# Routing logits taken out of the output product: VectorE sums of finished rows, TensorE for the last four tiles

## The chip, the cores and the metric

The kernel runs on one core of a Trainium2 chip, as one program. The metric is the device time of one execution in microseconds (us), lower is better; the figure for a kernel is the median of its runs.

## The reference, cut to what matters

Three stages follow each other over 3072 tokens of width 384. An attention recurrence (4 batches, 8 heads of 48, 768 steps) gives `x`; a gated layer of inner width 1536 follows; then a top-1 mixture of 8 experts of inner width 1024.

```
x = (sigmoid(x @ w_gate) * (x @ w_val)) @ w_out                  # 384 -> 1536 -> 384
xn = x / (norm(x) + 1e-6);  en = expert_emb / (norm(expert_emb) + 1e-6)
logits = xn @ en.T / tau                                          # 8 logits for each token
expert_idx = argmax(logits);  gate_w = softmax(logits)[expert_idx]
out = gate_w * (relu(x @ w1[expert_idx]) @ w2[expert_idx])
```

What matters here are the 8 logits of each token: they are inner products of the finished row `x` with the 8 normalised embeddings.

## The kernel before, in words

**Tokens and groups.** The 3072 tokens are 24 chunks of 128. Two chunks make a group of 256 tokens; there are 12 groups, 0 to 11. Attention is done chunk by chunk. Groups 0 and 1 are done one at a time (`emit_gv`, tiles `pgv`), groups 2 to 11 in five pairs of 512 tokens (`emit_wide`, tiles `pgate`, `pval`, 512 columns a product).

**The gated layer.** The inner width is cut into 12 blocks f. For each block of a pair TensorE makes the gate (9 matmuls, L730) and the value (9 matmuls, L730); VectorE multiplies with the sigmoid (`sgw`, L743), ScalarE rounds the product to a high part (`gth`, L745), VectorE subtracts for the low part (`gtl`, L747). One block later `emit_out` (L767 to L777) multiplies with the output weights `wo` and adds into the PSUM tiles `o`, 6 matmuls for a group, 12 for a pair, over all 12 blocks. Here "step" means one block of a pair: gate, value, and the output product of the block before. A step has two ticks; the stages of attention for the chunks ahead are hung on ticks by the table `stages` (6 ticks a chunk).

**Where the logits come from.** `wo` holds for each block 384 output columns and 8 more: w_out times the normalised embeddings. So the 392-column output product gives the row and its 8 logits together. To make the 8 columns, `conv` transposes each unit of output weights on TensorE (`ptw`, L446; ScalarE copies them, L447) and multiplies the transposes with the embeddings (`pg`, L457; copied at L461, L462). That happens six times, in the first 126 us.

**The early stage.** Up to 163 us the chunks 0 to 8, groups 0 and 1, and the conversion of 18 units of 64-bit weights (`conv`: two ScalarE passes, two VectorE passes, a rounding and a subtraction) are emitted by a planner: each is a generator that says when it wants to be emitted (`CHUNK_AT`, `CONV_AT`, `GV_AT`, ...), and whether it needs a temporary tile (`avail["x"]`). The tables do not depend on how long anything takes.

**Routing.** When a group's 12 blocks are summed, `route_pick` (L779) copies the 8 logits and the row from PSUM (tile `xr`), sums the squares on ScalarE (L799), and finds the expert on VectorE. `route_rank` (L803) counts, with three small matmuls `pr`, how many tokens went to each expert before, and scatters the rows (`xs`, L818, by GpSimd's indirect DMA) to the experts' regions in DRAM. `first_rows` (L882) counts what each expert has up to the last pair, sorts the experts, and loads the first 336 rows of one expert, which `first_xT` (L899) transposes and `first_h` (L911) uses right after the last pair: eight hidden blocks of 9 matmuls of 336 columns that cover the last rows' way through DRAM. Then 112 more rows (`x`, L1356) come back from DRAM, are transposed (L1363) and used (L1368), and the experts' products `y` (L1286) follow.

**Queues.** SP issues the loads in program order: `ld` and `ldr` are the attention chunks (three buffers: two of `ldp`, one of `r2p`; chunk c + 3 is loaded when chunk c is done with, L360), `raw` the 64-bit weights, `wraw` the experts' weights.

Of the kernel before, what the change touches and what calls it, by code (L numbers as in the profile page):

```python
# [8 lines left out]
F32 = mybir.dt.float32  # L9
# [13 lines left out]
RW = 400  # L23
# [18 lines left out]
AT_ROWS = 5  # L42
# [5 lines left out]
IN_ORDER = 16.12  # L48
EMB_AT = 20.18
WARM = 12  # L50
WARM_WIDE = 6
# [8 lines left out]
def kernel(  # L60
# [33 lines left out]
    xs = dram.tile([E * REGION, RW], F32, name="xs")  # L94

# [31 lines left out]
    def wtile(nm):  # L127
        return wp.tile([P, 1568], F32R, tag="w", name=nm)
# [170 lines left out]
    if True:  # L299
# [54 lines left out]
        def load_chunk(c):  # L354
            if c % 3 == 2:
# [42 lines left out]
        def load_unit(n):  # L398
            kind, i = units[n]
            w = wp.tile([P, 768], I64, tag="w", name="raw", padded_shape=[P, 784])  # L400
# [13 lines left out]
        def conv(n):  # L414
# [23 lines left out]
            wv = w.rearrange("p (f l c) -> p f l c", f=2, l=2)  # L438
            xv = x.rearrange("p (f c) -> p f c", f=2)
            nc.scalar.activation(wv[:, :, 0, 0:384], xv, AF.Copy)  # L440
            yield CONV_T[2], ("x", 1)
# [7 lines left out]
            lo.tensor_tensor(wv[:, :, 1, 0:384], xv, wv[:, :, 0, 0:384], op=ALU.subtract)  # L449
            avail["x"] += 1  # L450
            yield CONV_T[4], "en"

            pgs = ps_gv.tile([P, 2, P // E, E], F32, tag="gv", name="pg")
            pg = pgs[:, :, 0]
            for f in range(2):
                for k in range(3):
                    nc.tensor.matmul(  # L457
                        pgs[:, f], xT[:, f, k, :], enT[:, k, :].unsqueeze(1).to_broadcast([P, P // E, E]),
                        start=(k == 0), stop=(k == 2),
                    )  # L460
            nc.scalar.activation(wv[:, :, 0, 384:392], pg, AF.Copy)  # L461
            nc.vector.tensor_tensor(wv[:, :, 1, 384:392], pg, wv[:, :, 0, 384:392], op=ALU.subtract)  # L462
# [4 lines left out]
        embt = tmpp.tile([E, DM], F32, tag="x", name="embt")  # L467
        nc.sync.dma_start(out=embt, in_=emb)
        taut = c1.tile([E, 1], F32, name="taut")
        nc.sync.dma_start(out=taut, in_=tau.broadcast_to([E, 1]))  # L470
# [25 lines left out]

        def embeddings():
            esq = tmpp.tile([E, DM], F32, tag="x", name="esq")
# [9 lines left out]
            nc.vector.tensor_scalar(embt, embt, es[:, 5:6], None, op0=ALU.mult)  # L508
            pe = ps_gv.tile([P, 3, E], F32, tag="gv", name="pe")
# [211 lines left out]
        scores = {}  # L721

# [56 lines left out]
        def route_pick(g):  # L779
            xr = rtp.tile([P, 2 * RW], F32, tag="xr", name="xr").rearrange("p (t c) -> p t c", t=2)  # L780
            sq = tmpp.tile([P, DM], F32, tag="x", name="sq")
            lg = xr[:, :, 384:392]
            for t in range(2):
                nc.scalar.activation(lg[:, t], po[g][t][:, 384:392], AF.Copy)
# [10 lines left out]
            nc.gpsimd.memset(xr[:, :, 394:RW], 0.0)  # L795
            nc.gpsimd.tensor_copy(xr.bitcast(I32)[:, :, 393], tokid[:, 2 * g:2 * g + 2])
            for t in range(2):
# [211 lines left out]
        def rank_due(n):  # L1009
            for r in ranks:  # L1010
                r[0] -= 1
# [496 lines left out]
```

## Time and profile before

| | |
|---|---|
| median of 3 runs | 832.94 us (832.31 to 834.7) |
| the profiled execution | 836.85 us, its span 835.1 us, granted TensorE clock 0.982 |
| TensorE busy | 811.8 us, 97% of the span |
| VectorE busy | 414.5 us, 50% |
| ScalarE, GpSimd busy | 323.2 us (39%), 213.2 us (26%) |
| DMA | 99.85 MB, mean 120 GB/s |

Busy time is the union of an engine's instructions. The chain of waits follows the work that ended last back in time; its pieces are listed in order of time. A tile's name stands left of the arrow, what it is made from on the right. Clock figures are shares of 2.4 GHz.

### The profile page before, as it was taken

Reading aid. Unit: us, or ns where it says so; the run is one execution under the profiler, and the core shown is the slowest. Engines: PE = TensorE matmul, PEld = TensorE weight load, DVE = VectorE, ACT = ScalarE, POOL = GpSimd, SP = SyncE. Lnnn points to the kernel's source line nnn. Section 1 sums busy time; section 2 is a strip of 40 time slices with the busy share of each in tenths; the row PEclk is TensorE's granted clock in tenths of the full one; section 3 lists DMA queues with packets and bytes.
Section 4 is the critical chain, followed back from the end, with each engine's and each line's share of the span. In section 5 each row is a group of like instructions: output and inputs, shape, how many; then the busy total and the mean of one; then the engine's idle time right before and its main releaser. Section 6 shows DMA issues by size and latency. Waiting matters only on the chain.

```text
span 835.1 us, 16946 instructions
## 1 busy us (share of the span) xinstructions
PE 811.8 (97%) x6955; PEld 727.0 (87%) x6955; DVE 414.5 (50%) x913; ACT 323.2 (39%) x698; POOL 213.2 (26%) x247
## 2 busy tenths in 40 slices
PE   6899989999999999999999999999999999999997
PEld 5788989878888888888888888888999998899997
DVE  7998764533334333434353324343474554556650
ACT  6586743311223212321231224333364454555541
POOL 5612023653333433335141100100210102102202
PEclk8699999999999999999999999999999999999999
DMA  9568733312121222122211001610366466465401
GB/s 355 196 240 289 236 118 113 137 41 67 58 68 58 86 78 67 58 87 77 68 58 30 21 10 57 195 61 20 105 215 222 131 218 229 128 219 160 143 11 54
DMA packets 35357, 99.85 MB, mean 120 GB/s; under 512 B 4337, under 2 KB 18401, under 8 KB 32329
## 3 DMA queue, kind: packets, MB, share of 16 engines
q1 hardware_dynamic: 31639, 88.77, 31.6%
q0 software_dynamic: 3632, 9.93, 3.3%
q8 instruction: 56, 0.92, 0.4%
q14 instruction: 28, 0.23, 0.1%
q10 hardware_dynamic: 2, 0.00, 0.0%
HBM read 80.94 MB, written 16.27 MB: 116 GB/s over the span
## 4 chain that ended last, share of the span: by engine, by line
PE 76%; issue 12%; DMA 4%; DVE 3%; POOL 2%; ACT 1%; another core or an unknown queue 0%; POOLq 0%; SPq 0%; ACTq 0%
PE o L775 18%; PE pval L730 15%; PE pgate L730 15%; PE y L1286 7%; PE ph L924 7%; PE pgv L730 4%; PE py L647 3%; DMA ldr<-in_att_dram 2%; PE py L627 2%; DMA ld<-in_att_dram 2%; POOL out_dram L1329 1%; PE pg L457 1%; PE py L604 1%; PE pt L1251 1%; PE ph L1368 1%
## 5 line engine op out<-in xcount | busy, mean ns | idle before, releaser
L730 PE MATMUL pval<-xt,gv 128*128 128x512 f32 x540 | 135.8, 395 | 0.0
L730 PE MATMUL pgate<-xt,gv 128*128 128x512 f32 x540 | 134.6, 393 | 0.0
L775 PE MATMUL o<-wo,gth 128*128 128x392 f32 x480 | 128.2, 348 | 0.0
L730 PEld LDWEIGHTS pval<-xt,gv 128*128 128x128 f32 x540 | 100.2, 188 | 22.3 <-issue 0.4
L924 PE MATMUL ph<-xk,we 128*128 128x384 f32 (+6 forms) x576 | 116.9, 350 | 0.0
L730 PEld LDWEIGHTS pgate<-xt,gv 128*128 128x128 f32 x540 | 100.7, 188 | 18.0
L743 DVE TENSOR_TENSOR sgw<-pval,sgw 128x512 f32<-128x512 f32 x60 | 41.5, 691 | 139.3 <-PE pval L730 132.7
L924 PEld LDWEIGHTS ph<-xk,we 128*128 128x128 f32 x576 | 102.8, 188 | 6.0 <-issue 1.2
L1286 PE MATMUL y<-we,ht 128*128 128x384 f32 (+1 forms) x528 | 102.0, 340 | 0.0
L745 ACT ACTIVATE gth<-sgw 128x512 fp32r<-128x512 f32 x60 | 37.9, 632 | 146.8 <-DVE sgw L743 139.5
L739 ACT ACTIVATE sgw<-pgate 128x512 f32<-128x512 f32 x60 | 36.3, 605 | 146.8 <-PE pgate L730 138.1
L1286 PEld LDWEIGHTS y<-we,ht 128*128 128x128 f32 (+1 forms) x528 | 92.1, 187 | 1.0
L775 PEld LDWEIGHTS o<-wo,gth 128*128 128x128 f32 x480 | 87.6, 190 | 4.3
L775 PE MATMUL o<-wo,gtl 128*128 128x392 f32 x240 | 82.3, 343 | 0.0
L1329 POOL DMA_INDIRECT out_dram<-yo,xrow x26 | 26.6, 1022 | 173.6 <-ACT yo L1326 161.5
L747 DVE TENSOR_TENSOR gtl<-sgw,gth 128x512 fp32r<-128x512 f32 x60 | 46.7, 778 | 37.9 <-ACT gth L745 37.2
L844 DVE TENSOR_TENSOR we<-wraw,we 128x768 fp32r<-128x768 f32 x64 | 61.0, 957 | 8.3 <-ACT we L841 6.4
L929 DVE SCALAR_TENSOR_TENSOR ht<-ph,ht 128x384 fp32r<-128x384 f32 (+1 forms) x56 | 31.9, 569 | 64.6 <-ACT ht L928 60.1
L928 ACT ACTIVATE ht<-ph 128x384 fp32r<-128x384 f32 (+1 forms) x56 | 28.2, 503 | 85.6 <-PE ph L924 79.8
L730 PE MATMUL pgv<-xt,gv 128*128 128x256 f32 x432 | 59.0, 289 | 0.0
L730 PEld LDWEIGHTS pgv<-xt,gv 128*128 128x128 f32 x432 | 55.8, 194 | 0.4
L841 ACT ACTIVATE we<-wraw 128x768 fp32r<-128x768 f32 x64 | 53.3, 838 | 5.6 <-PE pval L730 2.9
(251 smaller groups left out, 1073.3 us busy)
## 6 DMA issues: line engine op xcount, KB each, us to landing
wraw<-in_wex_dram SPq DMA_DIRECT2D x64, 384.0 KB
ld<-in_att_dram SPq DMA_DIRECT2D x15, 1152.0 KB
raw<-in_wgv_dram SPq DMA_DIRECT2D x12, 768.0 KB
ldr<-in_att_dram SPq DMA_DIRECT2D x8, 1152.0 KB
w2f<-in_wex_dram SPq DMA_DIRECT2D x8, 768.0 KB
xs<-zt SPq DMA_DIRECT2D x8, 750.0 KB
raw<-in_wout_dram SPq DMA_DIRECT2D x6, 768.0 KB
xrow<-xs SPq DMA_DIRECT2D x6, 600.0 KB
```

The lines of the kernel that those rows point to most:

```text
L730: nc.tensor.matmul(pg, a, x[:, k, b, :], start=(n == 0), stop=(n == 8))
L739: nc.scalar.activation(sg, p0, AF.Sigmoid)
L743: nc.vector.tensor_tensor(sg, p1, sg, op=ALU.mult)
L745: nc.scalar.activation(hi, sg, AF.Copy)
L747: q = nc.vector.tensor_tensor(lo, sg, hi, op=ALU.subtract)
L775: nc.tensor.matmul(po[g][t], gt[a][:, ts_], w[:, f % 2, b, :], start=(f == 0 and n == 0), stop=(f == NF - 1 and n == 2))
L841: q = nc.scalar.activation(w[:, 0:768], r, AF.Copy)
L844: nc.vector.tensor_tensor(w[:, 768:1536], r, w[:, 0:768], op=ALU.subtract)
L924: nc.tensor.matmul(ph, a, x[:, k, b, :], start=(n == 0), stop=(n == 8))
L929: nc.vector.scalar_tensor_tensor(ht[:, 1, :], ph, 0.0, ht[:, 0, :], op0=ALU.max, op1=ALU.subtract)
L1286: nc.tensor.matmul(yo[e, t], ht[:, a, :], b, start=(f == 0 and n == 0), stop=(f == XF - 1 and n == 2))
L1329: q = nc.gpsimd.indirect_dma_start(out=out, out_offset=bass.IndirectOffsetOnAxis(ap=xrow[e][t].bitcast(I32)[:, 393:394], axis=0), in_=o, i ...
```

## The change

- `wo` loses the 8 columns; `emit_out` multiplies with 384 columns, and `conv` of an output unit makes no transposes and no products with the embeddings.
- `embeddings` loads its input itself, later (`EMB_AT` 20.18, then `EMB_T` 6.0), and writes the normalised embeddings to DRAM (`embd`). After the early stage SP loads them back to all 128 partitions (`embb`, 8 x 384 numbers a partition, into the third chunk buffer). From chunk 9 on the chunks have two buffers, and are loaded two chunks ahead.
- For groups 0 to 9, `route_rows` copies the row and sums the squares, and `route_dots` queues 16 VectorE products with a sum (128 x 384, `scalar_tensor_tensor` with `accum_out`: one for each of two tiles and eight experts), then the pick. Each tick takes some from that queue by the table `DOTS`: 10 in 6 ticks, in the last pair 4 in each tick. The first of a tick is held behind all earlier VectorE work.
- For groups 10 and 11 the rows are transposed on TensorE (`pty`, 12 transposes) and multiplied with the embeddings (`pl`, 12 matmuls of 8 columns), between the blocks of `first_h`; their ranks come after block 3.
- `first_rows` stands at block 7 of the last pair in place of 5, when all earlier groups have been ranked.

```diff
-AT_ROWS = 5
+AT_ROWS = 7
+RANK = 1
+DOTS = ((2, 3, 3, 2, 0, 0), (4, 4, 4, 4, 4, 4))
...
-            xT = tmpp.tile([P, 2, 3, P], F32, tag="x", name="xT")
-            for f in range(2):
-                pt = ps_gv.tile([P, 3, P], F32, tag="gv", name="ptw")
-                for k in range(3):
-                    nc.tensor.transpose(pt[:, k, :], xv[:, f, k * P:(k + 1) * P], ident)
-                nc.scalar.activation(xT[:, f], pt, AF.Copy)
...
-            pgs = ps_gv.tile([P, 2, P // E, E], F32, tag="gv", name="pg")
...
+            nc.sync.dma_start(out=embd, in_=embt)
...
-                po[g] = [ps_o.tile([P, 392], F32, tag=f"o{g % 2}{t}", name=f"o{t}") for t in range(2)]
+                po[g] = [ps_o.tile([P, DM], F32, tag=f"o{g % 2}{t}", name=f"o{t}") for t in range(2)]
...
+        def route_dots(g):
+            xr = route_rows(g)
+            for i in range(2 * E):
+                t, e = divmod(i, E)
+                dots.append(lambda t=t, e=e: nc.vector.scalar_tensor_tensor(
+                    prod, xr[:, t, 0:DM], 1.0, embb[0][:, e], op0=ALU.mult, op1=ALU.mult,
+                    accum_out=xr[:, t, 384 + e:385 + e],
+                ))
+            dots.append(lambda: ranks.append([tick + RANK, route_pick(g, xr)]))
...
+        def AFTER(c):
+            return 3 if c < EARLY else 2
...
+        t = r2p.tile([P, 3072], F32, tag="r2", name="embb")
+        nc.sync.dma_start(out=t, in_=embd.rearrange("e c -> (e c)").partition_broadcast(P))
...
+            n = min(DOTS[tick >= 24 * (len(WIDE) - 1)][tick % 6], len(dots))
...
         for f in range(XF):
             first_h(f)
+            if f == 0:
+                turned = [route_turn(xr, t, n) for n, (g, t, xr) in enumerate(tiles)]
+            elif f == 1:
+                for n, (g, t, xr) in enumerate(tiles):
+                    route_logits(xr, t, n, turned[n])
+                picks = [route_pick(g, xr) for g, xr in ends]
+            elif f == 3:
+                for p in picks:
+                    route_rank(*p)
```

Three places of the order show what moves. The first is SP's queue at the end of the early stage, first before, then now (`xt` are small copies of attention results, `ld` and `ldr` chunks):

```order
L360 DMA ld<-in_att_dram 128x2304
L360 DMA ldr<-in_att_dram 128x2304
L710 DMA xt<-xp_204 16x2x256 x3
L360 DMA ld<-in_att_dram 128x2304 x2
L710 DMA xt<-xp_204 16x2x256 x6
```

```order
L364 DMA ld<-in_att_dram 128x2304
L1140 DMA embb<-embd 128x3072
L700 DMA xt<-xp_203 16x2x256 x3
L364 DMA ld<-in_att_dram 128x2304 x2
L700 DMA xt<-xp_203 16x2x256 x6
```

The embeddings' load takes the place of a chunk's, behind the load of another chunk.

The second is VectorE in the third step of the last pair (`sgw` and `gtl` belong to the gated layer, `we` is the split of an expert's weights, `rs` a pick), first before, then now:

```order
L743 TENSOR_TENSOR sgw<-pval,sgw 128x512
L747 TENSOR_TENSOR gtl<-sgw,gth 128x512
L844 TENSOR_TENSOR we<-wraw,we 128x768
```

```order
L734 TENSOR_TENSOR sgw<-pval,sgw 128x512
L786 SCALAR_TENSOR_TENSOR prod,xr<-xr,embb 128x384 x2
L864 TENSOR_TENSOR we<-wraw,we 128x768
L738 TENSOR_TENSOR gtl<-sgw,gth 128x512
L786 SCALAR_TENSOR_TENSOR prod,xr<-xr,embb 128x384 x4
L813 TENSOR_REDUCE rs<-xr 128x2
L786 SCALAR_TENSOR_TENSOR prod,xr<-xr,embb 128x384
L815 TENSOR_TENSOR rs<-xr,rs 128x16
```

Seven sums and two operations of a pick now stand between two products of the gated layer.

The third is TensorE behind the last output product, up to the transposes of the 112 rows (`ph` are blocks of `first_h`, `pr` the ranks), first before, from the first rank, then now, from the first block:

```order
L807 MATMUL pr<-cum_97,ones 128x16
L924 MATMUL ph_6280<-xk,we 128x336 x3
L808 LDWEIGHTS U
L808 MATMUL pr<-oh,U 128x16
L809 LDWEIGHTS ones
L809 MATMUL pr<-oh,ones 128x8
L924 MATMUL ph_6280<-xk,we 128x336 x4
```

```order
L945 MATMUL ph_6252<-xk,we 128x336 x9
L795 MATMUL pty<-ident,xr 128x128 x6
L945 MATMUL ph_6288<-xk,we 128x336 x5
L795 MATMUL pty<-ident,xr 128x128 x6
L945 MATMUL ph_6288<-xk,we 128x336 x4
L806 MATMUL pl<-enT,yT 128x8 x12
L945 MATMUL ph_6335<-xk,we 128x336 x9
L945 MATMUL ph_6347<-xk,we 128x336 x9
L827 LDWEIGHTS ones
L827 MATMUL pr<-cum_98,ones 128x16
```

The ranks stood inside the first two blocks; now transposes, logits and four blocks come ahead of them, and 12 products `y` stand between the last block and the transposes of the 112 rows, where one did.

## Rows read from the trace of the kernel before

**Rows 1.** The page's part 1: busy us, share of the span, instructions.

```profile
PE 811.8 (97%) x6955; PEld 727.0 (87%) x6955; DVE 414.5 (50%) x913; ACT 323.2 (39%) x698; POOL 213.2 (26%) x247
```

**Rows 2.** Busy time by stretch: us, then PE, PEld, DVE, ACT, POOL, clock, DMA.

```profile
40.00:50.00 10.00, 9.59 (x97) 8.84 (x95) 9.55 (x16) 9.33 (x22) 2.58 (x2) 1.00 0.68 264
...
90.00:100.00 10.00, 10.00 (x74) 9.75 (x73) 7.82 (x14) 6.78 (x15) 0.94 (x1) 1.00 0.80 263
...
300.00:400.00 100.00, 100.00 (x910) 85.92 (x908) 38.24 (x87) 23.80 (x56) 39.19 (x38) 1.00 0.19 63
```

**Rows 3.** The chain of waits, early stage: start us, us, what.

```profile
72.78 0.55 PE ptw L446 x3
...
73.85 1.36 PE pg L457 x12
...
88.56 1.34 PE pg L457 x12
...
101.28 0.87 PE pg L457 x6
...
103.13 0.86 PE pg L457 x6
...
121.32 0.55 PE ptw L446 x3
...
123.15 2.66 PE pg L457 x12
```

**Rows 4.** Stretch by instructions of tile pg: PE, PEld, DVE, ACT, clock, DMA.

```profile
121.00:126.00 5.00, 2.73 (x12) 2.54 (x12) 0.00 (x0) 0.15 (x1) 0.66 0.00 0
```

**Rows 5.** The chain of waits: a chunk's load, and products of both widths.

```profile
108.42 7.73 DMA ld<-in_att_dram
...
167.95 2.15 PE o L775 x12
170.10 2.09 PE pgate L730 x9
...
626.85 2.09 PE y L1286 x12
```

**Rows 6.** Groups of instructions by form: busy us, mean ns, then idle before.

```profile
L844 DVE TENSOR_TENSOR we<-wraw,we 128x768 fp32r<-128x768 f32 x64 | 61.0, 957 | 8.3 <-ACT we L841 6.4 <-issue 0.7
...
L743 DVE TENSOR_TENSOR sgw<-pval,sgw 128x512 f32<-128x512 f32 x60 | 41.5, 691 | 139.3 <-PE pval L730 132.7 <-PE pr L809 6.6
...
L425 DVE SCALAR_TENSOR_TENSOR x<-x,raw 128x768 int32<-128x768 int32 x18 | 17.7, 992 | 1.9 <-ACT x L421 1.9
...
L799 ACT ACTIVATION_READ_ACCUMULATOR sq<-o 128x1 f32 x24 | 6.1, 254 | 0.0
...
L792 DVE TENSOR_REDUCE rs<-rs 128x2 f32<-128x16 f32 x12 | 2.1, 171 | 0.4
```

**Rows 7.** VectorE in order of time, the first two wide steps: start us, us.

```profile
165.37 1.08 DVE L747 TENSOR_TENSOR gtl<-sgw,gth 128x512 fp32r<-128x512 f32 x1 [0.70 <-ACT gth L745]
168.06 0.69 DVE L743 TENSOR_TENSOR sgw<-pval,sgw 128x512 f32<-128x512 f32 x1 [1.61 <-PE pval L730]
```

**Rows 8.** SP's queue in order of time, end of the early stage.

```profile
156.88 0.51 SPq L360 DMA_DIRECT2D ld<-in_att_dram  x1
159.88 0.34 SPq L360 DMA_DIRECT2D ldr<-in_att_dram  x1
```

**Rows 9.** All engines in order of time, behind the last output product.

```profile
575.29 0.42 PEld L905 LDWEIGHTS pt<-ident,first 112*128 112x128 f32 x3
...
584.51 0.71 PE L924 MATMUL ph<-xk,we 128*128 128x336 f32 x3
...
587.18 0.98 POOL L818 DMA_INDIRECT xs<-xr,pi  x1 [57.65 <-ACT hm L928]
...
596.95 0.45 PE L1363 MATMUL pt<-ident,x 112*128 112x112 f32 x3
...
598.47 1.42 PEld L1368 LDWEIGHTS ph<-x0T,raw 128*128 128x128 f32 x12 [0.18 <-DVE hm L929]
```

More of the change, by code (lines that the diff above doesn't have):

```diff
@@ L94 @@
     xs = dram.tile([E * REGION, RW], F32, name="xs")
+    embd = dram.tile([E, DM], F32, name="embd")
     scatters = {}
@@ L127, in wtile @@
     def wtile(nm):
-        return wp.tile([P, 1568], F32R, tag="w", name=nm)
+        return wp.tile([P, 1536], F32R, tag="w", name=nm)
     def gates(pool, np_, nt, lg, sq, after=None):
@@ L354, in load_chunk @@
         def load_chunk(c):
-            if c % 3 == 2:
+            if c % 3 == 2 and c < EARLY:
                 t = r2p.tile([P, 3072], F32, tag="r2", name="ldr")[:, 0:2304]
@@ L399, in load_unit @@
             kind, i = units[n]
-            w = wp.tile([P, 768], I64, tag="w", name="raw", padded_shape=[P, 784])
+            w = wp.tile([P, 768], I64, tag="w", name="raw")
             if kind == "gv":
@@ L495 @@
         enT = cst.tile([P, 3, E], F32, name="enT")
+        prod = c1.tile([P, DM], F32, name="prod")
+        embt = prod[0:E]
+        taut = c1.tile([E, 1], F32, name="taut")
+        embb = []
         def embeddings():
+            nc.sync.dma_start(out=embt, in_=emb)
+            nc.sync.dma_start(out=taut, in_=tau.broadcast_to([E, 1]))
+            yield EMB_T[0], ("x", 1)
             esq = tmpp.tile([E, DM], F32, tag="x", name="esq")
@@ L882, in first_rows @@
         def first_rows():
+            assert not dots and not ranks
             cum = cums[LAST % 3]
@@ L999 @@
         ranks = []
+        ends = []
         def drain(n):
@@ L1006, in drain @@
                     if f == NF - 1:
-                        ranks.append([2 + i, route_pick(g + i)])
-        def rank_due(n):
-            for r in ranks:
-                r[0] -= 1
-            while ranks and ranks[0][0] <= n:
-                route_rank(*ranks.pop(0)[1])
+                        if g < LAST:
+                            route_dots(g + i)
+                        else:
+                            ends.append((g + i, route_rows(g + i)))
         steps = []
@@ L1058, in at_stage @@
                     list(warm_up(WARM_WIDE))
-                if c + 3 < NCH:
-                    load_chunk(c + 3)
+                if c != EARLY - 1 and c + AFTER(c) < NCH:
+                    load_chunk(c + AFTER(c))
         def early_gv(g):
@@ L1070, in early_gv @@
                     emit_out(g, f - lag)
-            ranks.append([2, route_pick(g)])
-        def embed():
-            yield 0.0, ("x", 1)
-            embeddings()
-            avail["x"] += 2
-            done.add("en")
+            route_dots(g)
         done = set()
-        avail = {"x": 2}
+        avail = {"x": 3}
         def met(need):
@@ L1094 @@
             plan(CONV_AT[n] if n < 2 else CONV_AT[2] + (n - 2) * CONV_AT[3], units[n], conv(n))
-        plan(EMB_AT, "emb", embed())
+        plan(EMB_AT, "emb", embeddings())
         plan(INIT_AT[0], "init", init_slots())
@@ L1121 @@
             load_units(min((n for n in range(len(units)) if units[n] not in done), default=len(units)) + AHEAD)
+        t = r2p.tile([P, 3072], F32, tag="r2", name="embb")
+        nc.sync.dma_start(out=t, in_=embd.rearrange("e c -> (e c)").partition_broadcast(P))
+        embb.append(t.rearrange("p (e c) -> p e c", e=E))
         tick = 0
+        dotted = [len(nc.cur_bb.bb.instructions)]
         def at_tick():
-            if not open_y:
-                rank_due(0)
+            if not open_y and ranks and tick > ranks[0][0]:
+                route_rank(*ranks.pop(0)[1])
             for c, st in sorted(stages.get(tick, [])):
                 at_stage(c, st)
+            n = min(DOTS[tick >= 24 * (len(WIDE) - 1)][tick % 6], len(dots))
+            vector = lambda a: [q for q in nc.cur_bb.bb.instructions[a:] if q.engine == mybir.EngineType.DVE]
+            ahead = vector(dotted[0]) if n else []
+            first = len(nc.cur_bb.bb.instructions)
+            for _ in range(n):
+                dots.pop(0)()
+            if n:
+                for r in ahead:
+                    follow(vector(first)[0], r)
+                dotted[0] = first
         for g, f, wide in steps:
@@ L1154 @@
         drain(0)
-        rank_due(99)
+        tiles = [(g, t, xr) for g, xr in ends for t in range(2)]
+        turned = []
         for f in range(XF):
             first_h(f)
+            if f == 0:
[7 more added lines that the diff above has]
+                    route_rank(*p)
         q = nc.vector.tensor_scalar(lim[:, 0, :], wd, W_MIN, None, op0=ALU.is_ge)
@@ L1294, in load_rest @@
             for q in range(2):
-                w = wp.tile([P, 4, DM], F32, tag="w", name="w2f", padded_shape=[P, 4, 392])
+                w = wp.tile([P, 4, DM], F32, tag="w", name="w2f")
                 nc.sync.dma_start(
```

59 lines of the change are left out of this document (31 added, 28 removed).

## The prediction

> **What bounds the kernel now.** I read the page's part 1 first, then the busy time by stretch, then the chain of waits, and last the order of time where the change moves something. TensorE is busy for 97% of the span [rows 1]; from 300 to 400 us it never stops, while VectorE is busy for 38% and GpSimd for 39% [rows 2]. So in the wide stage only TensorE's own work counts, and VectorE has room. The early stage is different: from 40 to 50 us VectorE is as full (9.55 of 10 us) as TensorE (9.59), from 90 to 100 us TensorE is full and VectorE has 2.2 us left in 10 [rows 2]. Behind the last output product a third thing bounds: the last rows' way through DRAM. The first scatter starts at 587.18 us and the transposes of the 112 rows at 596.95, just where the eight blocks of `first_h` that began at 584.51 run out [rows 9]. So the cover there is used up to the last microsecond.
>
> The profiled execution took 836.85 us, 3.9 above the median of 832.94; the sum is made against it and carried over to the median. About 0.3%, 2.5 us, is what a measurement of this kernel can tell from no change.
>
> **The change, part by part.**
>
> *Narrower output product.* Twelve products of 392 columns take 2.15 us, twelve of 384 columns take 2.09 on the same engine at the same clock [rows 5]. I take 0.05 a dozen, between these rows' 0.06 and the 0.044 that the ratio of the columns gives. There are 60 dozens in the wide stage and 12 in groups 0 and 1: 72 x 0.05 = **-3.6 us**, with ends -3.2 and -4.3. All of it is on TensorE, which nothing else holds up there.
>
> *No transposes, no products with the embeddings, six units.* On the chain of waits after 72 us stand products of 1.36, 1.34, 0.87, 0.86 and 2.66 us and two of the transposes of 0.55 each [rows 3], together 8.2 us. The last product is dear because the granted clock is 0.66 around it [rows 4], against 1.00 elsewhere. What lies before 72 us I cost at nothing: VectorE covers it [rows 2]. After that VectorE's 2.2 us in 10 are enough for most of what TensorE frees, and the chain from 121 us on has no conversion left. I take **-8 us**. The ends: -3.5, if VectorE holds the stretch up to 105 us where it is and only the pieces at 121 and 123 count; -12, if transposes off the listed rows and VectorE's shorter waits come on top. SP's write of `embd` waits for VectorE, and weight loads stand behind it; a delay there pushes towards the first end. ScalarE's copies that go, and the chunk loads that come two chunks ahead, I cost at nothing: a load takes 7.73 us [rows 5], a chunk's turn is three steps of some 6.3 us (gate and value at 2.09 each, and 2.15 [rows 5]), and GpSimd, which needs the chunk first, is busy for 39% [rows 2]. If that cover were gone, GpSimd's products would come late, and attention's with them.
>
> *The embeddings' load.* It stands where SP issued a chunk at 159.88, behind a chunk (128 x 2304 numbers, 1152 KB) issued at 156.88 [rows 8]. It moves 128 x 3072 numbers, 1536 KB; at the chunk's 7.73 us for 1152 KB [rows 5] the two end 18 us after 156.88 one behind the other, some 14 if they go faster than that one row. I take 171.5 us. VectorE's first sum stands behind `gtl` at 165.37, and the next `sgw`, begun at 168.06 [rows 7], stands behind three sums. So `sgw` comes some 5.4 us late; TensorE needs its PSUM tile back one output and one gate product later, less its own 0.69 us: 2.15 + 2.09 - 0.69 = 3.55 us. **+2 us**, with ends 0 and +5.
>
> *The sums.* 160 of them, and no row shows one. The nearest row is VectorE's operation of the same kind with two 4-byte operands from SBUF, 768 wide: 0.99 us [rows 6]. At the difference to the 0.69 of a 512-wide product [rows 6] half the width would take about 0.55. The reading of the sum is the unknown: ScalarE's takes 0.25 [rows 6], a small VectorE operation 0.17 [rows 6], the lower end is nothing. I take 0.65 a sum, ends 0.55 and 0.80. In the wide stage a chunk's turn has 10 sums, 6.5 us, beside VectorE's 38%: hidden, by idle time that TensorE leaves. In the last pair it is tight. There a step lasts 6.33 us, and four steps in a row hold 27 sums, four products and four subtractions of 0.69, five splits of 0.96 [rows 6] and 11 small operations of 0.17 to 0.2: 17.6 + 5.5 + 4.8 + 2.1 = 30 us against 25.3. VectorE is then 4.7 us late where 3.55 are free, and `gtl` stands behind two sums and a split: **+2 us**, ends 0 and +5. The count, two steps (12.7 us) later than before, is cheap itself, but its loads stand behind the last scatters in SP's queue, ahead of a weight that VectorE's splits wait for; it is in the upper end. At pair ends ScalarE's copy of a row waits for a scatter two groups back that is now late; nothing taken, up to +2.
>
> *Behind the last output product.* TensorE gets 12 transposes at 0.14 (three weight loads took 0.42) and 12 logit products at 0.235 (six products of the same 4-byte kind took 1.42 in weight loads) [rows 9]: 1.7 + 2.8 = 4.5 us. The way of the rows gets longer by more. Before, the first scatter came 2.7 us after the first block began, the 112 rows 9.7 us later [rows 9]. Now copies, transposes, logits, pick and four blocks of some 1.45 us stand ahead: 4.5 + 4.3 x 1.45 + 1.2 for the pick and the ranks = about 12 us to the first scatter, 9.3 later. TensorE can use it for the 4.5 us and for 11 more products `y` at 0.174 [rows 5], 1.9 us, that it would make anyway; it then waits for about 2.9 us. Net 9.3 - 1.9 = **+7.4 us**. The ends: +4.5, if the wait is covered; +9.5, if the wait also costs clock, as the pause before 121 us did (rows 4's 0.66, 2.66 us for a product that took 1.36 [rows 3]).
>
> Sum: -3.6 - 8 + 2 + 2 + 7.4 = -0.2 us, 836.65 for the profiled execution, **832.7 us** for the median. The forecast: what the early stage gains, the tail takes back.
>
> **A rule against the change.** VectorE's operation with two 4-byte operands from SBUF takes 0.99 us for 768 elements [rows 6], about the pace of the split of the same width with its 0.96, so as long as nothing is summed it runs at full speed. The Trainium skill's page "Vector Engine (DVE) Microarchitecture Reference", under "Points that are easy to get wrong", says that this operation with two sources in SBUF that are not bf16 runs at half the throughput, since both read ports are taken and none is left for the accumulator. By that rule the sums would cost the 12 us more of the last rival below, by the row the 2 us above; the trace does not show the rule, and no run here has the operation with a sum.
>
> **The rivals.**
> *The early stage gives more, the tail takes less (faster).* -11 early, -3.6, +1 for load and sums, +5.5 in the tail: -8, 825 us. For it: the chain runs through TensorE from 72 us on [rows 3]. Against: VectorE is nearly as full [rows 2], and the tail's cover was used up before [rows 9]. 0.34.
> *VectorE holds the early stage (slower).* Conversion keeps its passes on VectorE, which has no idle time at 40 us [rows 2]; if its waits do not shrink after 72 us, only the pieces after 121 us count. Early -3.5, the rest as taken: +4.3, 837 us. It decides where VectorE stays over 95% busy up to 100 us. Beside it the range's ends of load, sums and tail. 0.25.
> *A sum takes as long as the 768-wide row, 1.0 us (slower).* The four steps of the last pair come to 27 + 5.5 + 4.8 + 2.1 = 39.4 us against 25.3, 14 late of which 3.55 are free; and the steps with six sums come to 6 + 1.4 + 1 for attention's operations, over their 6.33 us and what attention adds on TensorE, some 0.3 us for each of 14 chunks. 10.5 + 4 in place of 2: +12.3, 845 us. 0.05, because the row of 0.99 us has twice the elements [rows 6].
> *The order is other than it reads.* The order shows the products gone and the sums placed, so this has no chance of its own.
>
> **How the numbers follow.** The forecast, within 2.5 us of no change: 0.36, the likeliest, since it needs none of the terms at its end. The faster rival, with the part of the forecast's spread that falls below 830.4: 0.34. The two slower ones together: 0.30. The range reaches down to 823.5, a little past the faster rival's 825, and up to 842, where the slower rival's 837 meets the upper ends of the load, the sums or the tail; the case of 1.0 us a sum lies outside.
>
> **What would show it.** Right: twelve output products at 2.10 us; the first `pgate` 7 to 9 us earlier; a sum of 0.6 to 0.7 us; VectorE waiting for `embb` for some 5 us once; 9 to 10 us more between the first block and the transposes of the 112 rows, with a pause of TensorE of about 3 us. Wrong: an early stage as long as before, a sum of 0.8 us or more, TensorE pauses at each pair's end, or no pause before the 112 rows.

## The result and the profile after

The changed kernel takes 824.16 us (median of 4 runs, 821.06 to 825.67) against 833.66 us of the kernel before beside it (4 runs, 832.31 to 834.70): the ratio is 0.9882 with a 95% interval of 0.9848 to 0.9916, so it is 9.5 us or 1.2% faster. The forecast was 832.7 us, no change. The time came out at the faster rival's 825 us, inside the stated range but only 0.7 us above its lower end.

Both profiled executions can be cut at the same three places in TensorE's order: the first output product of the wide stage, the first block of `first_h`, and expert 1's first product. The stretches add up to the span.

| kernel (profiled execution) | up to first wide output product | wide stage | first block to expert 1 | rest | span |
|---|---|---|---|---|---|
| before | 167.79 | 416.72 | 36.31 | 214.28 | 835.1 |
| changed | 156.36 | 408.42 | 45.00 | 214.12 | 823.9 |
| difference | -11.43 | -8.30 | +8.69 | -0.16 | -11.2 |

The early stage gave more than the forecast had. The wide stage gave 8.3 us, where the forecast's terms for it come to about +1 (-3.0 for the narrower products, +2 for the embeddings' load, +2 for the sums). The tail took a little more than forecast.

**The sums cost almost nothing.** The page's first part of the changed kernel: VectorE's busy time went from 414.5 to 513.1 us, TensorE's fell from 811.8 to 798.7.

```profile
PE 798.7 (97%) x6883; PEld 714.4 (87%) x6883; DVE 513.1 (62%) x1233; ACT 317.7 (39%) x659; POOL 223.0 (27%) x247
```

The stretches of [rows 2] in the changed kernel (PE, PEld, DVE, ACT, POOL busy, granted clock, DMA share, GB/s):

```profile
40.00:50.00 10.00, 8.51 (x129) 7.44 (x126) 8.30 (x21) 6.11 (x16) 0.96 (x2) 0.56 0.33 122
90.00:100.00 10.00, 9.43 (x112) 8.70 (x112) 9.98 (x18) 5.81 (x12) 0.94 (x1) 1.00 0.99 350
300.00:400.00 100.00, 99.88 (x951) 85.79 (x944) 65.64 (x175) 24.49 (x56) 36.47 (x35) 1.00 0.22 75
```

From 300 to 400 us VectorE has 66 us of work instead of 38, and TensorE lost 0.12 us. From 90 to 100 us it is VectorE that is full now, and TensorE has 0.6 us left. From 40 to 50 us TensorE's clock is 0.56 now, where it was 1.00: TensorE waits there for the embeddings, which are made later (1.52 us up to 39.70, 1.49 us up to 48.75).

VectorE's groups, with the sum (busy us, mean ns, then idle before) and the reading of its accumulator:

```profile
L786 DVE SCALAR_TENSOR_TENSOR prod<-xr,embb 128x384 f32<-128x384 f32 x160 | 102.1, 638 | 3.6 <-DMA embb<-embd 1.1
L786 DVE DVE_READ_ACCUMULATOR prod<-xr,embb 128x1 f32 x160 | 13.0, 81 | 0.0
```

VectorE in order of time at the first sums, then GpSimd in the same 12 us:

```profile
156.38 0.56 DVE L786 SCALAR_TENSOR_TENSOR prod<-xr,embb 128x384 f32<-128x384 f32 x1 [1.07 <-DMA embb<-embd]
156.87 0.08 DVE L786 DVE_READ_ACCUMULATOR prod<-xr,embb 128x1 f32 x1
156.98 0.56 DVE L786 SCALAR_TENSOR_TENSOR prod<-xr,embb 128x384 f32<-128x384 f32 x1
...
158.07 0.68 DVE L734 TENSOR_TENSOR sgw<-pval,sgw 128x512 f32<-128x512 f32 x1
...
161.88 1.27 DVE L786 SCALAR_TENSOR_TENSOR prod<-xr,embb 128x384 f32<-128x384 f32 x1
```

```profile
161.52 1.22 POOL L575 TENSOR_TENSOR Am<-near,sd 128x512 f32<-128x512 f32 x1 [5.33 <-DVE sd L563]
162.71 1.60 POOL L551 TENSOR_TENSOR ld<-ld,tabs 128x512 f32<-128x512 f32 x1
```

A sum takes 0.56 us and 0.08 for the reading, 0.60 from one to the next; the mean of all 160 is 0.64, since one that meets GpSimd's work takes longer, here 1.27. The embeddings' load was issued at 148.41 and VectorE waited 1.07 us for it. `sgw` at 158.07 stands behind three sums; its product ended at 156.5, where the chain below goes over to the output products, so it came some 1.5 us late. That lies inside the 3.55 us that the prediction had free, and TensorE did not pause.

**The early stage.** The chain of waits of the changed kernel, early stage and first wide steps (start us, us, what):

```profile
101.03 2.15 PE pgv L721 x18
103.18 0.86 PE py L637 x48
...
106.86 2.08 PE o L766 x12
...
114.30 0.42 PE py L617 x10
...
119.86 2.35 PE pgv L721 x18
...
156.52 2.10 PE o L766 x12
```

Twelve output products take 2.10 us instead of the 2.15 of [rows 5]. And from 101 to 132 us the chain runs through TensorE alone. The kernel before had the chunk's load of [rows 5] there, from 108.42 us on. Its chain, ahead of that load and behind it:

```profile
107.46 0.90 PE py L647 x48
...
116.29 1.98 POOL ld L556
118.27 0.47 POOL Am L585
...
118.76 0.77 DVE Am L613 x2
...
121.86 0.51 PE py L627 x10
...
133.92 5.68 DMA ldr<-in_att_dram
```

The change issues these two loads at 104.14 and 123.22 us. So of the 11.4 us, 4.3 are gained by the first of them, 6.4 between the two, and 0.7 from the second to the first wide output product.

*Up to the first load.* By the chain it is issued when the 48 attention products `py` above are done. They start at 107.46 us in the kernel before and at 103.18 in the changed one, with the same work ahead of them: 78 matmuls of output products and 270 of gate and value in both. Up to 72 us nothing was gained (28 and 126 of these, before 30 and 126). So the columns' work that stood from 72 to 105 us gave nearly all that its pieces promised. VectorE is almost never idle there now (9.98 of 10 us from 90 to 100): it used up the room that [rows 2] show.

*Between the loads.* The same ten products `py` start at 121.86 and at 114.30 us, so 3.3 us more are gained by then. TensorE in the kernel before, behind the load, has two groups of transposes that go with the columns, and waits for VectorE ahead of each:

```profile
119.91 0.55 PE L446 MATMUL ptw<-ident,x 128*128 128x128 f32 x3 [1.29 <-DVE sg L760]
121.32 0.55 PE L446 MATMUL ptw<-ident,x 128*128 128x128 f32 x3 [0.86 <-DVE sg L760]
```

These `sg` stand on VectorE behind `Am`, that stands behind GpSimd's `Am`, and that behind GpSimd's first work on the chunk (`ld`, 116.29 above), which waited for the load. VectorE waited for the load too. Its first operation on the chunk, before and then now:

```profile
116.17 1.22 DVE L559 TENSOR_TENSOR ld<-ld,tabs 128x1024 f32<-128x1024 f32 x1 [2.06 <-DMA ld<-in_att_dram]
```

```profile
109.31 1.22 DVE L549 TENSOR_TENSOR ld<-ld,tabs 128x1024 f32<-128x1024 f32 x1
```

Now it starts 5.2 us after the load's issue and does not wait; before, it started 7.75 us after, and waited. GpSimd's order differs as well: now `Am` stands ahead of its work on the chunk.

```profile
109.34 1.55 POOL L575 TENSOR_TENSOR Am<-near,sd 128x192 f32<-128x192 f32 x1 [3.57 <-DVE sd L563]
110.86 1.02 POOL L546 TENSOR_TENSOR ld<-ld 128x384 f32<-128x384 f32 x1
```

So the two waits of TensorE, 2.15 us, are gone, and with them the 1.1 us of the transposes. Whether the shorter load or GpSimd's order took the waits away, no run shows. The other 3.1 us up to the second load are in the main the 2.66 us of the columns' product at 123.15 [rows 3].

**The tail.** TensorE in order of time behind the last output product; it answers to [rows 9]:

```profile
564.78 1.54 PE L945 MATMUL ph<-xk,we 128*128 128x336 f32 x9
566.16 0.82 PE L795 MATMUL pty<-ident,xr 128*128 128x128 f32 x6
...
569.08 2.74 PE L806 MATMUL pl<-enT,yT 128*128 128x8 f32 x24
571.68 3.01 PE L945 MATMUL ph<-xk,we 128*128 128x336 f32 x18
574.53 0.18 PE L827 MATMUL pr<-cum,ones 128*128 128x16 bf16 x1
...
581.06 2.31 PE L1326 MATMUL y<-we,hm 128*112 128x384 f32 x12 [0.48 <-PE pf L1208]
586.19 0.48 PE L1403 MATMUL pt<-ident,x 112*128 112x112 f32 x3 [2.83 <-DMA x<-xs]
...
587.38 2.86 PE L1408 MATMUL ph<-x0T,raw 128*128 128x112 f32 x12
```

GpSimd's first scatter, and SP's load of the 112 rows:

```profile
576.87 0.98 POOL L838 DMA_INDIRECT xs<-xr,pi  x1 [44.56 <-DVE pi L836]
```

```profile
583.62 0.35 SPq L1396 DMA_DIRECT2D x<-xs  x1
```

The first scatter stands 12.09 us behind the first block (before 2.67), the transposes of the 112 rows 21.41 us behind it (before 12.44). TensorE waits 0.48 and 2.83 us, and the products behind take 2.86 us where the same twelve took 1.42 in weight loads and 1.59 as products before. The stretches there show why (the number behind POOL's is the granted clock):

```profile
586.00:588.00 2.00, 1.81 (x10) 1.53 (x11) 0.51 (x1) 0.00 (x0) 0.19 (x1) 0.85 0.96 249
588.00:590.00 2.00, 2.00 (x12) 2.00 (x11) 0.27 (x1) 0.26 (x1) 0.00 (x0) 0.50 1.03 222
```

**The wide stage.** Of its 8.30 us, 4.82 come from one step, cut here from one value product to the next: the fourth lasts 12.70 us before and 7.88 now. VectorE in order of time in the kernel before, in that step:

```profile
180.02 0.17 DVE L816 CAST pi<-rs 128x2 int32<-128x2 f32 x1
182.79 0.35 DVE L640 TENSOR_TENSOR T<-T,py 128x192 f32<-128x192 f32 x1 [2.61 <-remote]
```

The ranks of groups 0 and 1 are made there, both in the step in which a chunk's attention begins: TensorE makes the ranks' `pr` between pieces of the attention's `py`, VectorE then waits 2.61 us for something that the profile can't name, TensorE pauses twice for 0.4 to 0.5 us, and its clock falls to 0.50 for the twelve output products behind (3.89 us instead of 2.15). The changed kernel makes these ranks from its sixth step on, one group at a time. The forecast had no term for this.

### The profile page after: what moved, and what is told of

Read it like the earlier page. It is cut to its first block, busy times and chain, and to the rows that moved or that the text cites. A ratio compares the mean times of both kernels' runs of the same rounds, so it can differ in the third digit from the quotient of the medians.

```text
span 823.9 us, 17081 instructions
## 1 busy us (share of the span) xinstructions
PE 798.7 (97%) x6883; PEld 714.4 (87%) x6883; DVE 513.1 (62%) x1233; ACT 317.7 (39%) x659; POOL 223.0 (27%) x247
## 4 chain that ended last, share of the span: by engine, by line
PE 76%; issue 12%; DVE 6%; POOL 3%; ACT 1%; DMA 1%; POOLq 0%; ACTq 0%; DVEq 0%
PE o L766 17%; PE pval L721 15%; PE pgate L721 15%; PE y L1326 7%; PE ph L945 6%; PE pgv L721 5%; PE py L637 3%; PE py L617 2%; POOL out_dram L1369 2%; PE py L594 1%; DVE x L429 1%; DVE x L430 1%; PE warm L376 1%; DVE gv L438 1%; PE ph L1408 1%
## 5 line engine op out<-in xcount | busy, mean ns | idle before, releaser
L766 PE MATMUL o<-wo,gth 128*128 128x384 f32 x480 | 125.0, 341 | 0.0
L786 DVE SCALAR_TENSOR_TENSOR prod<-xr,embb 128x384 f32<-128x384 f32 x160 | 102.1, 638 | 3.6 <-DMA embb<-embd 1.1
L766 PE MATMUL o<-wo,gtl 128*128 128x384 f32 x240 | 80.9, 337 | 0.0
L575 POOL TENSOR_TENSOR Am<-near,sd 128x512 f32<-128x512 f32 (+4 forms) x24 | 26.3, 1094 | 154.4 <-DVE sd L563 123.9
L864 DVE TENSOR_TENSOR we<-wraw,we 128x768 fp32r<-128x768 f32 x64 | 61.1, 957 | 10.1 <-ACT we L861 8.3
L721 PE MATMUL pgv<-xt,gv 128*128 128x256 f32 x432 | 60.8, 299 | 2.0 <-DVE xt L690 2.0
L721 PEld LDWEIGHTS pgv<-xt,gv 128*128 128x128 f32 x432 | 58.1, 205 | 3.2 <-DVE xt L690 2.5
```

Source lines behind the costliest of these rows:

```text
L721: nc.tensor.matmul(pg, a, x[:, k, b, :], start=(n == 0), stop=(n == 8))
L766: nc.tensor.matmul(po[g][t], gt[a][:, ts_], w[:, f % 2, b, :], start=(f == 0 and n == 0), stop=(f == NF - 1 and n == 2))
L786: dots.append(lambda t=t, e=e: nc.vector.scalar_tensor_tensor(prod, xr[:, t, 0:DM], 1.0, embb[0][:, e], op0=ALU.mult, op1=ALU.mult, accum_ ...
L864: nc.vector.tensor_tensor(w[:, 768:1536], r, w[:, 0:768], op=ALU.subtract)
```

## The experiments

All stretches below are cut as in the table above. The runs were made on three chips, on which the kernel before took 833.69 us (the first four runs below), 828.24 (the next four) and 832.23 (the last four). So times are compared on one chip.

**The kernel before once more**, no edit.

> The kernel before, unchanged, for a second profile. In the first one its fourth wide step lasted 12.70 us, against 7.88 in the changed kernel: VectorE sat idle for 2.6 us there and TensorE's clock fell. One-off theory: the stall belongs to that one execution; the fourth wide step now lasts 7.2 to 8.0 us and the stretch from the first wide output product to the first block of first_h some 412 us instead of 416.6. Rival: it belongs to the order of the kernel before, and the change removed it; 12 to 13 us again, 416 to 417 us for the stretch.

Measured: 835.65 us; the fourth wide step 12.64 us, the wide stage 416.61. The stall came again, so the one-off theory falls.

**The columns' work back in the early stage.**

```diff
+            xT = tmpp.tile([P, 2, 3, P], F32, tag="x", name="xT")
...
+                    nc.tensor.transpose(pt[:, k, :], xv[:, f, k * P:(k + 1) * P], ident)
+                nc.scalar.activation(xT[:, f], pt, AF.Copy)
...
+                    nc.tensor.matmul(
+                        pgs[:, f], xT[:, f, k, :], enT[:, k, :].unsqueeze(1).to_broadcast([P, P // E, E]),
...
+            nc.scalar.activation(cols[:, 0], pg, AF.Copy)
```

> The changed kernel with the transposes, the products with the embeddings and their copies back in the early stage (their result goes to a tile that nothing reads; the output products stay 384 wide, the routing stays with the sums). Theory: the early stage's gain of some 11 us is this work on TensorE and ScalarE; the time goes up by 8 to 11 us, to 832 to 835, and the first wide output product, at 156.5 us in the changed kernel, starts at 165 to 168. Rival: the gain comes from the other edits of the early stage (three temporaries free from the start, the embeddings loaded later): up by 0 to 3 us, 824 to 827, the first output product at 156 to 160.

Measured: 847.10 us, 1.018 of the kernel before (1.0137 to 1.0224). The first wide output product starts at 170.80, 14.4 us later than in the changed kernel; both lie above what the theory had. The work of the columns is enough for the whole gain. But the 14.4 us hold a wait that neither kernel has, in which the attention stands behind VectorE:

```profile
51.08 1.51 PE L657 MATMUL py<-Am,ld 64*64 64x64 f32 x16 [7.62 <-DVE Am L623]
```

So the run shows the direction, and not what the columns' pieces cost by themselves. The wide stage got 7.3 us longer too, which neither expectation had: 3.4 us in one step, the rest in 0.06 to 0.07 a step, mostly in the value products (2.10 instead of 2.04 us), which I can't explain. In the one step a chunk lands late; GpSimd, then TensorE in order of time:

```profile
301.62 1.30 POOL L572 TENSOR_TENSOR ld<-ld,tabs 128x512 f32<-128x512 f32 x1 [9.86 <-DMA ld<-in_att_dram]
```

```profile
308.79 0.18 PE L847 MATMUL pr<-cum,ones 128*128 128x16 bf16 x1 [1.82 <-DVE Am L623]
```

The same happened in the run with more TensorE work below, whose wide stage is that of the changed kernel (GpSimd waited 9.25 us there):

```profile
296.80 0.18 PE L828 MATMUL pr<-cum,ones 128*128 128x16 bf16 x1 [1.49 <-DVE Am L604]
```

So the cover of the chunks' loads, which are issued two chunks ahead now, is thin: one late load goes through GpSimd and VectorE to TensorE.

**The other edits of the early stage undone.**

```diff
         load_unit(0)
+        nc.sync.dma_start(out=embt, in_=emb)
+        nc.sync.dma_start(out=taut, in_=tau.broadcast_to([E, 1]))
...
-            nc.sync.dma_start(out=embt, in_=emb)
-            nc.sync.dma_start(out=taut, in_=tau.broadcast_to([E, 1]))
-            yield EMB_T[0], ("x", 1)
+            yield 0.0, ("x", 1)
...
-        avail = {"x": 3}
+        avail = {"x": 2}
```

> The changed kernel with the embeddings loaded as early as before and the planner starting with two temporaries free instead of three until they are done. Theory (the gain is the work of the columns): within 2.5 us of the changed kernel's 824. Rival (the gain comes from these edits): up by 5 to 10 us, 829 to 834.

Measured: 824.82 us, as the theory has it. In the profile the early stage was 3.6 us shorter (152.74) and the tail 2.7 longer (47.67): the clock fell to 0.50 right behind the logit products, so that two blocks of `first_h` took 4.56 us instead of 3.01, and the wait for the 112 rows was 4.17 us instead of 2.83. With the embeddings early the clock from 40 to 50 us is 1.00.

**More products ahead of the 112 rows.**

```diff
+        for f in range(AHEAD_Y):
+            for t in range(3):
+                emit_y(0, f, t)
...
         pt = ps_t.tile([P, 3, ST], F32, tag="t", name="pt0")
```

> The changed kernel with 36 products y of the first three tiles, instead of 12, ahead of the transposes of the 112 rows. Theory: behind the last output product the change loses its time in TensorE's waits of 0.48 and 2.83 us for the late rows and in the clock that falls behind them (12 products of 112 rows took 2.86 us instead of 1.59): 24 products of 0.174 us cover 4.2 us, the waits and the fall go, down by 3 to 4.5 us, to 820 to 821. Rival: the chain behind the 112 rows (their products, relu, the fourth tile, weights) sets the end, so that later transposes give back what the cover gains: between 1 us down and 2 us up.

`AHEAD_Y` is 4. Measured: 827.34 us, nothing gained; the tail lasts 46.73 us. TensorE in order of time:

```profile
581.16 6.50 PE L1327 MATMUL y<-we,hm 128*112 128x384 f32 x36 [0.48 <-PE pf L1209]
587.69 0.48 PE L1411 MATMUL pt<-ident,x 112*128 112x112 f32 x3
591.92 1.03 PE L1292 MATMUL pt<-ident,xrow 120*128 120x120 f32 x4 [3.75 <-DMA xrow<-xs]
```

The wait for the 112 rows is gone, and expert 1's rows, whose transposes came to stand right behind, are waited for in its place. Neither expectation had that.

**The same with those transposes kept behind the 112 rows' products.**

```diff
+                first = [q for q in nc.cur_bb.bb.instructions if q.engine == pe]
                 do_xT(1, f - 3)
+                then = [q for q in nc.cur_bb.bb.instructions if q.engine == pe][len(first):]
+                follow(then[0], first[-1])
```

> The earlier run with 36 products y ahead of the 112 rows gained nothing, since the next expert's transposes of its rows came right behind them on TensorE and waited 3.75 us for their load. Here they stand behind the 112 rows' products again. Theory (TensorE's waits for late rows and the clock behind them are the tail's loss): from the first block of first_h to expert 1's first product 40.5 to 42 us instead of the changed kernel's 45.0, the time 820 to 821.5. Rival (the chain of the 112 rows sets the end): 44.5 to 46 us, 823.5 to 825.

Measured: 818.27 us, 0.9876 of the kernel before (0.9855 to 0.9896). The changed kernel was not run on this chip, so the stretch decides: it is 42.05 us, and two runs on the same chip with the changed kernel's tail had 44.98 and 45.07. TensorE's waits and the clock behind them were the loss: 3 us came back. It would have been more, but for this (stretches, as above):

```profile
566.00:569.00 3.00, 3.00 (x29) 3.00 (x27) 1.25 (x5) 0.68 (x2) 0.00 (x0) 1.00 0.00 0
569.00:571.00 2.00, 2.00 (x10) 2.00 (x11) 1.51 (x13) 0.00 (x0) 0.00 (x0) 0.66 0.01 4
571.00:573.00 2.00, 2.00 (x9) 2.00 (x9) 0.91 (x4) 0.45 (x1) 0.00 (x0) 0.50 0.00 0
```

Right behind the twelve logit products of 8 columns the clock fell to its lower level, 1.2 GHz, without a pause of TensorE, and two blocks of `first_h` took 4.55 instead of 3.01 us:

```profile
569.08 4.55 PE L946 MATMUL ph<-xk,we 128*128 128x336 f32 x18
```

**The kernel before with later ranks.**

```diff
-            ranks.append([2, route_pick(g)])
+            ranks.append([LATER + g, route_pick(g)])
```

`LATER` is 6; the first scatter moved from 179.93 to 221.02 us.

> The kernel before, with nothing changed but that the ranks of groups 0 and 1 are made some four steps later, one at a time. Theory: its fourth wide step of 12.70 us is both groups' ranks in the step in which a chunk's attention starts (the PSUM tile of the ranks, VectorE's small operations, two pairs of scatters); the step falls to 7.9 to 8.5 us, the wide stage to 411.5 to 413, the time to 828 to 830. Rival (the stall has to do with something else of the early stage, the code or the loads there): the step stays at 12 to 13 us and the time within 2 us of the kernel before.

Measured: the fourth step lasts 7.91 us and the wide stage 410.46. VectorE in order of time, the row that waited 2.61 us:

```profile
177.96 0.35 DVE L641 TENSOR_TENSOR T<-T,py 128x192 f32<-128x192 f32 x1 [2.99 <-PE py L648]
```

With the ranks moved the step is as short as in the changed kernel. The time, though, was that of the kernel before beside it: 828.09 against 828.24 us (ratio 0.9986 to 1.0008). On this chip the kernel before was 5.4 us faster than on the first one, and no profile of it was taken here. An estimate: with the other three stretches as in this run's profile (166.29, 36.03 and 214.02 us), its median span of 826.5 us leaves 410.2 us for its wide stage, where this run has 410.46. So on this chip it probably had no such stall, and that the ranks' place makes the stall is not shown.

**More VectorE work, and more TensorE work, in the early stage of the changed kernel**, one at a time.

```diff
             lo.tensor_tensor(wv[:, :, 1, :], xv, wv[:, :, 0, :], op=ALU.subtract)
+            lo.tensor_tensor(wv[:, :, 1, :], xv, wv[:, :, 0, :], op=ALU.subtract)
```

> The changed kernel with the subtraction of each of the six output weights made twice: six more VectorE operations of 0.95 us in the early stage. Theory (without the columns' work VectorE bounds the early stage, full from 45 to 106 us): up by 4 to 6 us, the first wide output product at 160.5 to 162 instead of 156.4. Rival (TensorE still bounds it): up by 0 to 1.5 us.

```diff
             lo.tensor_tensor(wv[:, :, 1, :], xv, wv[:, :, 0, :], op=ALU.subtract)
+            list(warm_up(9))
```

> The changed kernel with nine products of 128 columns at full 4-byte precision added behind each of the six output weights' subtractions, on data that is always there: some 2 us of TensorE each, 12 us in all, as much as the columns' own products and transposes, but with no copies and nothing that waits for them. Theory (VectorE bounds the early stage now, and what the columns cost was partly the time on TensorE and partly their copies and temporaries): up by 3 to 7 us. Rival 1 (TensorE time alone was the cost): up by 10 to 13 us. Rival 2 (all of it was copies, temporaries and order): up by 0 to 2 us.

Measured: the first wide output product at 158.62 and at 161.08 us, against 155.87 in the tail run on the same chip, whose early stage is unchanged. So 5.7 us of VectorE cost 2.75, and 12 us of TensorE cost 5.2, with a higher clock in its favour (0.91 from 40 to 60 us, against 0.74 in the tail run). The first of these is hardly more than the 2.5 us by which two executions of one kernel differ in this stage (below). The times are 822.94 and 830.23 us; they can't be held against the changed kernel, which was not run on this chip. It looks as if neither engine alone sets the end of this stage, and some half of what either gets more of shows. The first theory's 4 to 6 us was too much, the rival's 0 to 1.5 too little; the second theory's 3 to 7 held for the early stage.

**A third profile of the kernel before, and the changed kernel beside it.**

> The kernel before once more, for a profile beside the next runs. Two chips gave it medians of 833.7 and 828.2 us, and on the second the version with the late ranks took as long as the unchanged one. Theory (the stall in the fourth wide step belongs to the kernel before only where its run is the longer one): where the time is near 828 us that step lasts 7.3 to 8.5 us, where it is near 833 us 12 to 13 us. Rival: 12 to 13 us at a time near 828 too; then the difference of 5 us lies in another stretch.

> The changed kernel, unchanged, beside the kernel before on the same chip. Theory (11.4 us of the early stage and 3 us of the columns gained, 8.7 us lost in the tail, the stall of 4.8 us gained only where the kernel before has it): 9 to 11 us faster than a kernel before of about 833 us, 4 to 7 us faster than one of about 828 us. Rival (the stall plays no part in the times): 9 to 11 us faster in both cases.

Measured: the kernel before took 834.15 us in its profile and 832.23 in the median beside it; its fourth step lasted 10.97 us, this time without a fall of the clock. The changed kernel took 824.38 us, a ratio of 0.9906 (0.9884 to 0.9928): 7.9 us faster. The step is shorter where the gain is smaller, but 10.97 us lies outside what either expectation had, and 7.9 us below both. Its early stage ended at 153.85 us, 2.5 us earlier than in the first profile, so two executions can differ there by that much. Its tail took 43.48 instead of 45.00 us: TensorE waited 2.77 us for the 112 rows, and the clock stayed up behind the wait:

```profile
585.40:587.40 2.00, 2.00 (x19) 1.88 (x18) 0.55 (x2) 0.60 (x3) 0.00 (x0) 1.00 1.02 217
```

**A shorter tail, without and with the side edits undone.** The edits of the two tail runs above, and:

```diff
-                nc.scalar.activation(sq, po[g][t], AF.Square, accum_out=xr[:, t, 392:393])
...
+                for g, xr in ends:
+                    late_squares(xr)
-            elif f == 3:
+            elif f == 2:
                 for p in picks:
```

> The changed kernel with 36 products y ahead of the 112 rows, the next expert's transposes behind their products, ScalarE's copies of the last four tiles ahead of their squares, and the last two groups' ranks one block of first_h earlier. Theory (the tail's loss is TensorE's waits, and the way of the rows gets shorter): from the first block of first_h to expert 1's first product 40 to 42 us instead of 45.0, 3 to 5 us less time than the changed kernel in the same call. Rival (another wait takes over, or the clock falls behind the logit products of 8 columns as in the last such run): 43 to 45 us, 0 to 2 us less.

> The run before this one, with the embeddings loaded as early as before and two temporaries free at first, which made the early stage 3.6 us shorter in an earlier profile. If that gain is real and the tail no longer eats it: 2 to 4 us less than the run before this one, the first wide output product at 152 to 154 us instead of 156. If it was chance: within 1 us of it, 155.5 to 157 us.

Measured: 819.87 us (ratio to the kernel before 0.9832 to 0.9865) and 819.86 us (0.9814 to 0.9860). Both beat both kernels: 12.4 us under the kernel before, 4.5 under the changed kernel beside them. The stretch is 42.11 and 42.12 us, no shorter than without the earlier ranks: the clock fell behind the logit products again (0.50 from 572 to 574 us in the first), and so the first scatter, for all its shorter way, stands 12.93 us behind the first block. The side edits gave 2.5 us in the early stage of the profile and nothing in the median; since two executions of one kernel differ as much, that gain is not shown. For it speaks that the two profiles with the embeddings early have the first wide output product at 152.74 and 153.34 us, the five others with the changed kernel's early stage at 153.85 to 156.36.

## Where the prediction was right and where it was wrong, point by point

The time lies inside the stated range, but the forecast of no change did not come true, and no case came out as it was reasoned.

- *Narrower output product, -3.6*: right. 2.10 us a dozen for 2.15, 0.6 us in the early stage and 3.0 in the wide one.
- *No columns, -8*: right in kind, too small. It was -10.8 (-11.4 less the 0.6). The listed pieces before 105 us, 5.0 us of the 8.2, came out with about 4 us at the first load (4.3 less 0.3 for the narrower products), nearly as forecast: VectorE's room was enough for most of them, and the slower rival, by which VectorE holds that stretch, is refuted, though VectorE is over 95% busy there now. **The step that failed** is the sentence that costs the chunks' loads at nothing, since a chunk's turn covers a load. In the early stage of the kernel before that is not so: the chain of waits itself has two loads on it, from 108.42 and from 133.92 us, and behind the first TensorE waits 1.29 and 0.86 us. I used this load as a price and passed over where it stood. Between the two loads 6.3 us came where 3.2 were listed (again less the narrower products): 2.15 of the difference are these waits, which are gone, and 0.55 a group of transposes that was not listed. That the columns' work is the cause is shown by undoing the side edits, which took nothing of the gain away, and in its direction by putting the work back. What stands behind the load is read from the two traces; no run moved a load alone.
- *The embeddings' load, +2*: nothing. The two loads went through in 10.1 us (from the chunk's issue at 146.27 to the first sum at 156.38) where I had taken 14 to 18, and the 1.5 us by which `sgw` came late were covered.
- *The sums, +2 in the last pair*: a size that was near, 0.60 us for 0.65. The last 14 steps are 0.41 us shorter than before (86.72 for 87.13), where the narrower products alone give 0.7; that leaves 0.3 us for the sums and what else moved there. They are hidden elsewhere, as forecast. By the rule of the Trainium skill's page "Vector Engine (DVE) Microarchitecture Reference", section "Points that are easy to get wrong", half speed was due; the trace does not agree: 384 elements with the sum take 0.56 us, 768 without took 0.99 [rows 6].
- *The tail, +7.4*: right in its mechanism, a size off. Measured +8.7: 3.8 us of transposes and logits (I had 4.5), waits of 3.3 us (2.9), and 1.5 us of clock, which I had put into the upper end alone. In the execution in which the clock stayed up it was +7.2.
- *The wide stage*: **a term was missing**, the stall of 4.8 us in the fourth step. I knew that the ranks move, but costed only the late ones. The views were there: by stretches the granted clock was 0.91 from 180 to 200 us and 1.00 from 200 to 580, and VectorE's order of time had a wait whose releaser it can't name. In the profiles the step is long with the ranks there (12.70, 12.64 and 10.97 us) and short with the ranks moved (7.91 and, in the changed kernel, 7.88), but on the chip where I took the ranks away the time didn't move. So what makes the stall, and how much of it stands in the times, is open.

Added to the forecast's -0.2 us, these differences (-2.8 for the columns, -2 for the load, -1.7 for the sums, +1.3 for the tail, -4.8 for the stall) come to -10.2 of the -11.2 us between the two profiles; the last 1 us has no name.

The faster rival named 825 us. Its -11 for the early stage was right, but its tail of +5.5 was 3.2 us too low and it had no stall of 4.8 us; that its sum met the time is luck, since these two errors in the main cancelled.

## What to carry to other kernels

When work is taken off a chain of waits, look at every transfer that is still on it, and ask what will issue that transfer earlier and what waits behind it: a load that waits for its buffer moves with the work ahead of it, and the waits behind it can go. Look for single steps that last longer than their like before costing a change by means; a small helper's work (here perhaps two groups' ranks) that meets another stage's start can cost more than all its instructions. When a wait is covered by work moved ahead, check what the engine's order then puts behind it, since the next late transfer may take its place.

## What the runs showed of the hardware

- VectorE slows beside GpSimd: a sum of 0.56 us took 1.27 while GpSimd multiplied (161.52 to 164.31 us). The Trainium skill's page "SBUF — State Buffer", section "Who interferes with whom", says that a VectorE instruction with two inputs in SBUF contends with one of GpSimd's that reads SBUF; this trace agrees.
- TensorE's granted clock fell to 0.50 in four executions right behind twelve products of 8 columns, with TensorE busy all the time by its records, and in six others, with the same products, it did not (the two profiles of the changed kernel among them). Behind a wait of 2.7 to 4.2 us for late rows it fell in six of seven executions; in the seventh, behind 2.77 us, it stayed up. A fall cost about 1.5 us in the executions shown.
- Of 59 steps of the wide stage, 48 repeat to 0.01 us in the three profiles of the kernel before, on different chips, and 49 in the nine profiles with the changed kernel's wide stage. One of the others is the fourth step before, with the stall. So a step that differs from its like is worth a look.
